# Attention, FFN and gated convolution on one core: the instruction order from a list scheduler, and the first FFN matrix scaled in groups

## The chip, the cores and the metric

The kernel runs on one core of one Trainium2 chip. The metric is device time in microseconds, the median of the runs shown. In the texts PE is TensorE (matmuls), DVE is VectorE, ACT is ScalarE, POOL is GpSimd and SP is the queue from which every DMA is issued. L12 is line 12 of the kernel's file.

## The reference

Attention over 4 batches, 8 heads, 576 positions and head size 64, then a layer norm with a two-layer FFN, then a gated block with a causal convolution of 5 taps:

```python
q_rot, k_rot = rotate(q), rotate(k)                     # rotary embedding
scores = q_rot @ k_rot.T / sqrt(64)
attn = softmax(scores)                                  # maximum subtracted
x = (attn @ v) as (4, 576, 512)
xn = (x - mean) / sqrt(var + 1e-6) * g_ln
x = x + relu(xn @ w_ch1) @ w_ch2                        # 512 -> 2048 -> 512
gate = sigmoid(sum_k conv_w[k] * x shifted by 4 - k)
out = (gate * (x @ w_val)) @ w_out
```

The weights arrive as float64; the FFN's two are 8 MB each.

## The kernel before

Rows are cut in 18 tiles of 128 (tile n spans batches, which have four and a half tiles each). For every matrix product each operand is split into a high and a low half (fp16, or fp32r in the scores and the gated block), and three products, high by high, high by low and low by high, are added in PSUM.

*Attention.* There are 16 pairs of heads (4 batches by 4). `schedule_prep` loads q and k of a pair (L188), multiplies by the rotary tables (`mul`, L196), adds (`add`, L200), and writes the high half on ACT (`hi`) and the low half on DVE (`lo`). V is bounded by the maximum of its sums, scaled by a power of two and split (`vabs`, `vmax`, `vscale`, `vhi`, `vlo`). A score tile is 128 query rows of one head against 576 keys: six matmuls of 288 columns with 64 contraction rows (`a_scores`, L292). The two heads of a pair sit on partitions 0 to 63 and 64 to 127, and `a_scores` issues their matmuls in turn. The 64 rows that are left of a batch are done for both heads in one diagonal tile (`qd`). So a pair has nine tiles, 144 in all. Each goes through maximum (DVE, L297), exponential (ACT, L303), high half (ACT, L305), low half (DVE, L310), a DMA transpose (SP, L312) and the product with V (PE, L331 and L334). Two PSUM buffers hold scores. Batch 0 is cut by rows in three parts, 128, 128 and 320, each for all four pairs of heads; the other batches are done pair by pair.

*Weights.* Each FFN matrix comes in eight pieces of 1 MB (`Conv`): ACT and DVE make fp32 of float64 (L391, L395, L396), PE multiplies each piece with itself (L403) to bound the column norms, and one bound over all eight pieces gives one scale (`conv_scale`). Only then are the pieces scaled into high and low halves (`conv_hi`, L437, and `conv_lo`, L441). The hidden units are computed 512 at a time.

*FFN.* A row tile is normalised once all heads of its rows are done (`ln_a`, `ln_b`, `ln_d`). `f1` makes 512 hidden units in 48 matmuls of 128 columns (L520), `relu` and `hlo` split them, and `f2` adds them to the output in 12 matmuls of 512 columns (L548). The halves of the hidden units have four buffers.

*Gated block.* It goes by two row tiles: copy (L609), DMA transpose, copy (L612), high and low half (L617, L618), taps on DVE (L631), `val` (L645) and `proj` (L662).

*What sets the order.* The program is written in slots, one for each score tile. Steps are put on an agenda with a slot and a phase (`at`), and `run_slot` issues a slot's steps by phase. How many FFN steps a slot gets is a running credit (`F_0`, `F_MIN`, `F_MAX`). After that the framework's own scheduler moves instructions by its estimate of their times, one instruction at a time, so a step's instructions need not stay together. Loads are chained to stay in order (`load_in_order`, L80), and the last products are held behind the last FFN matmul (`late_pe`).

Of the kernel before, what the change touches and what calls it, by code (L numbers as in the profile page):

```python
# [26 lines left out]
LAG, LN_AHEAD = 5, 2  # L27
W1_A, W1_S, W2_A, W2_S, W_BR = -7, 2, 14, 2, 2
F_0, F_MIN, F_TAIL, F2_LAG = 0.4, 0.1, 0.8, 4
F_MAX = 0.6  # L30
STEP, X3, GT, GV, GAP_0, GAP_1, V_LEAD = 6, 1, 6, 1, 0, 0, 3
HS_0, HS_1, HS_2, LD_LEAD, RAW, KQ = 8, 4, 6, 4, 3, 2


def pow2_below_inverse(nc, pool, bound, name):

    m = pool.tile([128, 1], F32, name=name + "_m", tag=name + "_m", bufs=1)
    nc.vector.tensor_scalar(out=m, in0=bound, scalar1=1e-30, scalar2=1.02, op0=ALU.max, op1=ALU.mult)
    nc.vector.reciprocal(out=m, in_=m)
    r = pool.tile([128, 1], F32, name=name + "_r", tag=name + "_r", bufs=1)  # L40
    nc.vector.tensor_scalar(out=r.bitcast(I32), in0=m.bitcast(I32), scalar1=0x7F800000, scalar2=None, op0=ALU.bitwise_and)
    return r


def pow2_below_inverse_root(nc, pool, bound, name):

    m = pool.tile([128, 1], F32, name=name + "_m", tag=name + "_m", bufs=1)
    nc.vector.tensor_scalar(out=m, in0=bound, scalar1=1e-30, scalar2=1.05, op0=ALU.max, op1=ALU.mult)
# [3 lines left out]
    nc.vector.tensor_scalar(out=r, in0=r, scalar1=2.0 ** 63, scalar2=None, op0=ALU.mult)  # L52
    return r
# [3 lines left out]
def kernel(ctx: ExitStack, tc: tile.TileContext, qk, v, g_ln, w_ch1, w_ch2, w_val, conv_w, w_out, rope, eye, out):  # L57
# [13 lines left out]
    QX = S - 256  # L71
    KT = conv_w.shape[1] // (2 * KD)

    agenda = {}
    last_load = []

    def load_in_order(**kw):

        with tc.issue_after(last_load[-1]) if last_load else nullcontext():
            last_load.append(nc.sync.dma_start(**kw).ins)  # L80


    count = [0, -100]

    def at(i, phase, fn):
        count[0] += 1
        assert i >= count[1], (i, count[1])
        agenda.setdefault(i, []).append((phase, count[0], fn))

    def run_slot(i):  # L90
        count[1] = i
        now = agenda.setdefault(i, [])
        while now:
            e = min(now)
            now.remove(e)
            e[2]()
        del agenda[i]
        count[1] = i + 1

    EX, PRE, SC, LO, MX, F2, PV, F1, DV, AC, PO, LD = range(12)  # L100

    L = lambda es, name, bufs, **kw: es.enter_context(tc.tile_pool(name=name, bufs=bufs, side="left", reuse_waits="tile", **kw))
    R = lambda es, name, bufs, **kw: es.enter_context(tc.tile_pool(name=name, bufs=bufs, side="right", reuse_waits="tile", **kw))

# [16 lines left out]
    sW, sF, sA = ExitStack(), ExitStack(), ExitStack()  # L121
# [4 lines left out]
    scl = wpool.tile([128, 4], F32, name="scl")  # L126
    gab = wpool.tile([128, KD], F32, name="gab")
    gmax = wpool.tile([128, 1], F32, name="gmax")
    sg = wpool.tile([128, KD], F32, name="sg")
# [11 lines left out]
    kk = [ap_k.tile([128, 4 * S], F32, name="kk", tag="kq") for _ in range(2)]  # L141

# [24 lines left out]
    prep = [None] * len(parts)  # L167
    base = [next(j for j, y in enumerate(parts) if y[:2] == x[:2]) for x in parts]

    def slot_of(i):  # L170
        return i + GAP_0 * (i >= first[NP]) + GAP_1 * (i >= first[2 * NP])
# [4 lines left out]
    def schedule_prep(p, pool):  # L176
# [3 lines left out]
        st = prep[p] = {"x": [None, None]}  # L180

        two = base[p] != p

        def load(n):
            t = pool.tile([128, 2, S], F32, name="raw", tag="raw", bufs=RAW)
            st["r", n] = t[:, :, 0:S if n else nq]
            load_in_order(out=st["r", n], in_=qk[b, pr][:, n, :, slice(0, S) if n else slice(q0, q1)])

        def vload():
            st["vt"] = (pool if p < NP else ap_v).tile([128, 10, D], F32, name="vt", tag="vt", bufs=2 if p < NP else 1)  # L190
            load_in_order(out=st["vt"], in_=v[b, pr].rearrange("p c h d -> p (c h) d"))
# [10 lines left out]
        def hi(n):  # L202
            if b:
# [5 lines left out]
            elif two:  # L209
                st["x"][0] = ap_q.tile([128, 2, QX], F32R, name="qs", tag="qs", bufs=2)[:, :, 0:nq]  # L210
# [9 lines left out]
        def diag():  # L220
            if ts[0][0] is None:
                c = ts[0][1] - q0
                for h in range(2):
                    sl = slice(64 * h, 64 * h + 64)
                    nc.scalar.copy(out=qd[sl, :, sl], in_=st["x"][0].bitcast(F32)[sl, :, c:c + 64])

        def vabs():

            st["vh"] = ap_v.tile([128, 18, D + 1], F16, name="vh", tag="vh")
            nc.gpsimd.memset(st["vh"][:, :, D:], 1.0)  # L230
# [4 lines left out]
        def vmax():  # L235

            st["va"] = ps_h.tile([128, 128], F32, name="hp", tag="hp")
            nc.tensor.matmul(st["va"], upper(st["vb"]).to_broadcast([128, 128]), ident, start=True, stop=True)
            st["vm"] = ap_m.tile([128, 1], F32, name="vm", tag="vm", bufs=2)
            nc.vector.tensor_reduce(out=st["vm"], in_=st["va"], axis=AX.X, op=ALU.max)  # L240

        def vscale():
            r = pow2_below_inverse(nc, ap_m, st["vm"], "vs")
            sv = st["sv"] = ap_m.tile([128, 1], F32, name="sv", tag="sv")
            nc.vector.tensor_scalar(out=sv, in0=r, scalar1=2.0 ** 15, scalar2=None, op0=ALU.mult)
# [4 lines left out]
        def vlo():  # L250
            vh = st["vh"]
            vl = st["vl"] = ap_v.tile([128, 10, D], F16, name="vl", tag="vl")
            nc.vector.scalar_tensor_tensor(out=vl, in0=st["vt"], scalar=st["sv"], in1=vh[:, 0:10, 0:D], op0=ALU.mult, op1=ALU.subtract)  # L253
            nc.scalar.copy(out=vh[0:64, 10:18], in_=vh[64:128, 0:8])
            nc.scalar.copy(out=vh[64:128, 10:18], in_=vh[0:64, 2:10])

        i1 = slot_of(first[p])
        e = (slot_of(first[p - 1]) if p else -4) + LAG - V_LEAD * (p < NP)
        vplan = [] if two else [(e - 2, LD, vload), (e, EX, vabs), (e, LD, vmax), (e + 1, LO, vscale), (e + 1, AC, vhi), (e + 2, LO, vlo)]

        def chain(n, c):
# [74 lines left out]
    def a_out(g):  # L336
        ov = ovs.pop(g)
        n = len(groups[g])
        p = tiles[groups[g][0]][0]
        b, pr = parts[p][:2]  # L340
        xx = xs[b // 2]
        lead = tiles[groups[g][0]][1] is None
        w = n + lead
        rd = ap_m.tile([128, 6], F32, name="rd", tag="rd")
        nc.vector.tensor_scalar(out=rd[:, 0:w], in0=ov[:, 0:w, D], scalar1=1e-9 * P_SCALE, scalar2=prep_v(p)["sv"], op0=ALU.add, op1=ALU.mult)
        nc.vector.reciprocal(out=rd[:, 0:w], in_=rd[:, 0:w])
        if lead:
            p0 = 64 * (b % 2)
            for h in range(2):
                r = slice(64 * h, 64 * h + 64)  # L350
                nc.scalar.activation(out=xx[p0:p0 + 64, 4, (2 * pr + h) * D:(2 * pr + h + 1) * D], in_=ov[r, h, 0:D], func=ACTF.Copy, scale=rd[r, h:h + 1])
        m = (n - lead) // 2
        if m:
            t0 = ((b % 2) * S + tiles[groups[g][lead]][2]) // 128
            by_head = lambda x: x.rearrange("p (t h) d -> p t h d", h=2)
            nc.vector.tensor_tensor(out=xx[:, t0:t0 + m, 2 * pr * D:2 * (pr + 1) * D].rearrange("p t (h d) -> p t h d", h=2), in0=by_head(ov[:, 2 * lead:2 * lead + 2 * m, 0:D]), in1=by_head(rd[:, 2 * lead:2 * lead + 2 * m].unsqueeze(2).to_broadcast([128, 2 * m, D])), op=ALU.mult)

    for i in range(NS):
        j = slot_of(i)
        at(j, SC, lambda i=i: a_scores(i))  # L360
        at(j, MX, lambda i=i: a_max(i))
        at(j + 1, EX, lambda i=i: a_exp(i))
        at(j + 2, LO, lambda i=i: a_lo(i))
        at(j + LAG, PV, lambda i=i: a_pv(i))
    for g, ts in enumerate(groups):
        at(slot_of(ts[-1]) + LAG + 1, LO, lambda g=g: a_out(g))


    def upper(x):

        return x.bitcast(BF16).rearrange("p (n two) -> p n two", two=2)[:, :, 1]

    class Conv:

        def __init__(self, scratch, src, out, bound=None):
# [85 lines left out]


    fst = {}
    tail = {}  # L470
    fpool = {}

    def ffn_start():
# [332 lines left out]
```

## Time and profile before

| | us |
|---|---|
| median of 3 runs (lowest to highest) | 780.15 (778.78 to 783.21) |
| span of the profiled execution | 777.0 |
| PE busy | 709.5 |
| DVE busy | 605.7 |
| ACT busy | 432.0 |

The profiled execution shows its span, from the first to the last instruction; its time around the span is not given. A busy time is the union of an engine's instructions. Matmuls overlap in the pipeline, so a busy PE is not PE at its peak, and the spacing of blocks in the chain of waits says more than a matmul's mean. In the table by stretch the columns are the stretch and its length, each engine's busy time with its number of instructions, the granted TensorE clock, the busy share of the 16 DMA engines, and GB/s. In the groups by line they are line, engine, operation, tiles, shapes and count, then busy time and mean ns of one, then the idle time ahead and what ended it.

### The profile page before, as it was taken

The page shows a single profiled execution, that of the slowest core. Times are in us where ns is not written, and L with a number is a line of the kernel's source. Part 1 is how long each engine was busy: PE and PEld are TensorE (multiplying, and loading weights), DVE is VectorE, ACT ScalarE, POOL GpSimd, SP SyncE. Part 2 cuts the span into 40 slices and gives each one's busy share as a digit, 9 for nine tenths or more (in the row PEclk, how much of TensorE's full clock was granted, in tenths as well). Part 3 has the DMA queues.
Part 4 walks back from the last instruction along what each step waited for, and adds up shares of the span by engine and source line. Part 5 has one row for each costly group of instructions (what it writes and reads, how often), then busy time and mean ns, then how long its engine had stood idle before and what let it go on. Part 6 is the DMA issues. An engine that isn't in the chain of part 4 may idle for free.

```text
span 777.0 us, 19132 instructions
## 1 busy us (share of the span) xinstructions
PE 709.5 (91%) x7996; PEld 560.5 (72%) x7996; DVE 605.7 (78%) x1202; ACT 432.0 (56%) x749; POOL 15.4 (2%) x39
## 2 busy tenths in 40 slices
PE   2466777999999899999999999999999999999997
PEld 1345675686777778677777768777777778778886
DVE  6989999899788799766758886665688744659994
ACT  3678757877577667464545565564363322334553
POOL 0000000000000001000000100000100000000000
PEclk9999998999999999999999999999999999999999
DMA  7999897596898867775746676656475311202311
GB/s 251 300 268 273 252 232 157 102 184 118 173 185 179 146 126 119 162 142 96 155 73 145 113 159 115 98 84 93 79 242 83 42 21 35 55 1 59 97 63 55
DMA packets 225847, 103.62 MB, mean 133 GB/s; under 512 B 210528, under 2 KB 213600, under 8 KB 224736
## 3 DMA queue, kind: packets, MB, share of 16 engines
q1 hardware_dynamic: 225760, 102.39, 61.1%
q8 instruction: 63, 1.03, 0.6%
q14 instruction: 24, 0.20, 0.1%
HBM read 45.73 MB, written 4.72 MB: 65 GB/s over the span
## 4 chain that ended last, share of the span: by engine, by line
PE 58%; DVE 18%; DMA 15%; issue 4%; ACT 4%; SPq 1%; POOL 0%; ACTq 0%; DVEq 0%; POOLq 0%
PE acc L548 18%; PE hp L520 16%; PE sc L292 8%; PE po L662 5%; PE pv L645 5%; DMA pT<-p 4%; DMA raw<-in_qk_dram 4%; PE ov L331 4%; DVE nmx L297 3%; DVE p L310 2%; PE ov L334 2%; DVE raw L196 1%; DMA tx<-rope_sb 1%; DVE wall L396 1%; DMA r<-in_moe_w_val_dram 1%
## 5 line engine op out<-in xcount | busy, mean ns | idle before, releaser
L520 PE MATMUL hp<-xT,wall 128*128 128x128 f16 x3456 | 214.5, 220 | 2.8 <-DVE hl L538 1.3
L520 PEld LDWEIGHTS <-wall 128*128 128x128 f16 x3456 | 199.4, 98 | 17.7 <-issue 8.7
L548 PE MATMUL acc<-wall,hh 128*128 128x512 f16 x544 | 163.1, 381 | 0.2 <-DVE x L552 0.2
L303 ACT ACTIVATE p<-sc,nmx 128x576 f32<-128x576 f32 x144 | 103.9, 737 | 86.4 <-DVE nmx L297 82.8
L310 DVE SCALAR_TENSOR_TENSOR p<-p,p 128x576 f16<-128x576 f32 x144 | 106.8, 753 | 52.1 <-ACT p L305 51.6
L297 DVE TENSOR_REDUCE nmx<-sc 128x1 f32<-128x576 f32 x144 | 105.6, 751 | 8.1 <-PE sc L292 7.7
L305 ACT ACTIVATE p<-p 128x576 f16<-128x576 f32 x144 | 95.6, 679 | 27.7 <-DMA pT<-p 25.8
L548 PE MATMUL acc<-wall,hl 128*128 128x512 f16 x272 | 103.1, 379 | 0.3 <-DVE hl L538 0.3
L331 PE MATMUL ov<-vh,pT 128*128 128x65 f16 (+1 forms) x1296 | 90.3, 201 | 12.9 <-DMA pT<-p 3.8
L331 PEld LDWEIGHTS <-pT 128*128 128x128 f16 x1296 | 79.2, 101 | 25.0 <-issue 16.4
L548 PEld LDWEIGHTS <-hh 128*128 128x128 f16 x544 | 49.3, 98 | 53.0 <-issue 4.5
L538 DVE SCALAR_TENSOR_TENSOR hl<-hp,hh 128x512 f16<-128x512 f32 x68 | 46.5, 686 | 36.3 <-ACT hh L532 36.2
L292 PE MATMUL sc<-kq 64*128 64x288 f32 x576 | 71.8, 309 | 0.8 <-ACT p L303 0.7
L532 ACT ACTIVATE hh<-hp 128x512 f16<-128x512 f32 x68 | 40.0, 591 | 57.2 <-PE hp L520 56.9
L334 PE MATMUL ov<-vl,pT 128*128 128x64 f16 (+1 forms) x720 | 69.9, 201 | 1.3 <-DVE vl L253 1.2
L631 DVE SCALAR_TENSOR_TENSOR gt<-xT,cw,gt 128x256 f32<-128x256 f32 (+10 forms) x192 | 69.3, 423 | 0.2
L292 PEld LDWEIGHTS sc<-kq 64*128 64x128 f32 x576 | 55.6, 184 | 7.5 <-ACT p L303 1.3
L334 PEld LDWEIGHTS <-pT 128*128 128x128 f16 x720 | 54.3, 101 | 4.3 <-issue 0.3
L196 DVE TENSOR_TENSOR raw<-raw,rope_sb 128x1152 f32<-128x1152 f32 (+2 forms) x40 | 44.5, 1116 | 10.5 <-DMA raw<-in_qk_dram 10.5
L548 PEld LDWEIGHTS <-hl 128*128 128x128 f16 x272 | 26.6, 98 | 31.6 <-DVE hl L538 0.5
L662 PE MATMUL po<-woh,gv 128*128 128x512 f32 x144 | 48.4, 402 | 0.3 <-ACT x L665 0.3
L292 PE MATMUL sc<-kx,qs 64*128 64x288 f32 x144 | 32.9, 394 | 11.9 <-ACT p L303 11.0
(114 smaller groups left out, 930.9 us busy)
## 6 DMA issues: line engine op xcount, KB each, us to landing
raw<-in_qk_dram SPq DMA_DIRECT2D x28, 576.0 KB, 4.7
wall<-in_moe_w_ch_dram SPq DMA_DIRECT2D x8, 1024.0 KB, 7.7
kk<-in_moe_w_ch_dram SPq DMA_DIRECT2D x8, 1024.0 KB, 5.6
vt<-in_v_dram SPq DMA_DIRECT2D x16, 320.0 KB, 3.0
out_dram<-x SPq DMA_DIRECT2D x18, 256.0 KB, 2.2
pT<-p SPq DMA_TRANSPOSE x144, 3.6
r<-in_moe_w_val_dram SPq DMA_DIRECT2D x4, 512.0 KB, 6.0
r<-in_moe_w_out_dram SPq DMA_DIRECT2D x4, 512.0 KB, 4.6
```

The source lines that it names most:

```text
L196: nc.vector.tensor_tensor(out=a, in0=a, in1=t, op=ALU.mult)
L292: nc.tensor.matmul(live[i + e][:, half, 0:HS], lw[rows, a], xk[rows, k, half * HS:(half + 1) * HS], start=(n == 0), stop=(n == 2))
L297: nc.vector.tensor_reduce(out=nmx, in_=sc[:, :, 0:HS], axis=AX.XY, op=ALU.max, negate=True)
L303: nc.scalar.activation(out=p32.rearrange("p (e n) -> p e n", e=2), in_=sc[:, :, 0:HS], func=ACTF.Exp, bias=nmx)
L305: nc.scalar.activation(out=p16[:, 0], in_=p32, func=ACTF.Copy, scale=P_SCALE)
L310: nc.vector.scalar_tensor_tensor(out=p16[:, 1], in0=p32, scalar=P_SCALE, in1=p16[:, 0], op0=ALU.mult, op1=ALU.subtract)
L331: nc.tensor.matmul(o, pT[:, c], vh[:, 2 * c + hs:2 * c + hs + nh], start=(c == 0), stop=(c == 8))
L334: nc.tensor.matmul(o[..., 0:D], pT[:, c], vl[:, 2 * c + hs:2 * c + hs + nh], start=False, stop=False)
L520: nc.tensor.matmul(hp[:, j], w1[:, u, wl * 512 + o:wl * 512 + o + 128], xT[:, xl * KD + c], start=(i == 0), stop=(i == 3 * KD - 1))
L548: tail["last"] = nc.tensor.matmul(st["acc"], lw[:, j], w2[:, f + j, lo * 512:lo * 512 + 512], start=(f + j == 0 and i == 0), stop=(f + j = ...
L631: nc.vector.scalar_tensor_tensor(out=gt[:, c0:c1], in0=xT[:, c, HALO + c0 - s:HALO + c1 - s], scalar=col(KT - 1 - s), in1=gt[:, c0:c1], op ...
L662: nc.tensor.matmul(po, lw[:, d, sl], rx[:, d, :], start=(n == 0), stop=(n == 3 * KD - 1))
```

## The change

The slots, the agenda and the credit go. Every step is now registered with a planner (`Plan.step`): its engine, an assumed time, a rank, the steps it comes after, the buffers it takes and uses, and the bytes if it is a transfer. `Plan.run` plays the engines forward: of the engines it takes the one whose next step can start first, and on that engine, among the steps ready by then (within `NEAR`), the one of lowest rank. Attention steps rank by their tile, FFN steps rank behind them (f1 1000, f2 900), relu, layer norm and FFN output ahead of them, and val and proj ahead of f1 and f2. The list that results is written out under `tc.manual_schedule()`, so the instructions stand as the planner has them and the framework moves none. The diff in its core:

```diff
-    agenda = {}
-    def at(i, phase, fn):
-        agenda.setdefault(i, []).append((phase, count[0], fn))
...
+class Plan:
+    LAG = {"PE": 0.22, "DVE": 0.12, "ACT": 0.2, "POOL": 0.15, "SP": 1.9, "": 0.0}
+    RATE, NEAR, AHEAD = 313.0, 0.15, 2.0
...
+        while len(done) < len(self.steps):
+            best = None
+            for eng, xs in todo.items():
+                now = max(free.get(eng, 0.0), wire - self.AHEAD if eng == "SP" else 0.0)
+                can = [(r, x) for x in xs for r in [ready(x)] if r is not None]
+                if not can:
+                    continue
+                t = max(now, min(r for r, x in can))
+                x = min((x for r, x in can if r <= t + self.NEAR), key=lambda x: (x.rank, x.order))
+                t = max(t, ready(x))
+                if best is None or t < best[0]:
+                    best = (t, eng, x)
+            x.end = t + x.time
+            if x.size:
+                x.end = wire = max(wire, x.end) + x.size / self.RATE * 1e-3
...
+    TURN = 330000
+    dve = lambda n: 0.07 + n / 960
+    act = lambda n: 0.095 + n / 1200
...
+            x = plan.step(PE, 0.85 if h is None else 1.08, R_SC + i, lambda i=i: a_scores(i), after=..., takes=ss, ...)
...
+    order = plan.run(dict(kq=kkb))
+    with tc.manual_schedule():
+        for x in order:
+            x.fn()
```

Batches 0 and 1 are cut in rows, each part for all four pairs of heads before the next; batches 2 and 3 stay pair by pair:

```diff
         if b == 0:
-            cuts = [(c, c + 128, [(0, c), (1, c)]) for c in (0, 128)] + [(256, S, [(None, c4)] + [(h, c) for c in (256, 384) for h in range(2)])]
+            cuts = [(c, c + 128, [(0, c), (1, c)]) for c in (0, 128, 256)] + [(384, S, [(None, c4), (0, 384), (1, 384)])]
+        elif b == 1:
+            cuts = [(0, 192, [(None, c4), (0, 64), (1, 64)])] + [(c, c + 128, [(0, c), (1, c)]) for c in (192, 320, 448)]
```

The first FFN matrix is loaded in pieces of 1024 hidden units by 256 rows. Two pieces have a bound and a scale of their own; the hidden units of 512 have the scale of their group, and the second matrix takes the ratio of the group's scale to the least of the four (`s1`, `srt`, `s2`). The second matrix keeps one bound over its eight pieces. The safety factors of the bounds are all 1.08, applied once, and powers of two are multiplied in where the scale is used:

```diff
-        m = wpool.tile([128, 1], F32, name=f"wm{w}")
-        nc.vector.tensor_reduce(out=m, in_=bound[w], axis=AX.X, op=ALU.max)
...
+        ne = 1 if w else 4
+        per = 8 // ne
+        for e in range(ne):
...
+    def conv_turn(w, e):
+        nc.tensor.matmul(o, upper(m).to_broadcast([128, 128]), ident, start=True, stop=True)
...
+        r = pow2_below_inverse_root(nc, wpool, m, 1.08 if w else gmax, f"w{w}{e}")
+        if w == 0:
+            nc.vector.tensor_scalar(out=sg[:, e], in0=g_sb, scalar1=r, scalar2=ROOT * W1_SCALE, op0=ALU.mult, op1=ALU.mult)
```

So 16 halves of 512 columns are scaled for the first matrix where there were 8 of 1024. The arithmetic of the tiles, the buffers of scores, transposes and hidden units, and the number of matmuls in f1, f2, scores, value products, val and proj stay.

Three places show what moved. On PE, in attention, two heads of one pair before (`sc` are score tiles, `hp` a bound of V, `acc` the FFN output):

```order
L292 MATMUL sc_3316<-kq_2703 128x288 x6
L238 LDWEIGHTS vb_3311
L238 MATMUL hp_3357<-ident_62,vb_3311 128x128
L292 MATMUL sc_3317<-kq_2703 128x288 x6
L548 LDWEIGHTS hh_3313
L548 MATMUL acc_2825<-wall_72,hh_3313 128x512
```

and a pair in the changed order:

```order
L443 MATMUL sc_3587<-kx0_68,qs_3192 128x288
L443 MATMUL sc_3588<-kx0_68,qs_3192 128x288
L443 MATMUL sc_3587<-kx0_68,qs_3192 128x288
L443 MATMUL sc_3588<-kx0_68,qs_3192 128x288
L443 MATMUL sc_3587<-kx0_68,qs_3192 128x288
L443 MATMUL sc_3588<-kx0_68,qs_3192 128x288
```

Before, one head's six stand together and other work stands between the two heads in many pairs; now the twelve always alternate (the six rows above go on in the same way).

On DVE, in the start, around a scaling of the first matrix (`wall<-wall,sg`), before:

```order
L395 TENSOR_SCALAR wall<-wall 128x1024
L346 RECIPROCAL rd<-rd 128x2
L396 SCALAR_TENSOR_TENSOR wall<-kk,wall 128x1024
L356 TENSOR_TENSOR x_67<-ov,rd 128x128
L441 SCALAR_TENSOR_TENSOR wall<-wall,sg 128x2x512
L297 TENSOR_REDUCE nmx<-sc 128x1
L486 BN_STATS bs<-x_67 128x6
```

and now:

```order
L626 TENSOR_SCALAR sg<-g_sb,w_r 128x4
L627 TENSOR_SCALAR s_74<-w_r 128x1
L465 SCALAR_TENSOR_TENSOR p_432<-p_413,p_432 128x576
L308 TENSOR_TENSOR raw<-raw,rope_sb 128x2x128
L648 SCALAR_TENSOR_TENSOR wall<-wall,sg 128x512
L312 TENSOR_TENSOR raw<-raw 128x128
L448 TENSOR_REDUCE nmx<-sc 128x1
L648 SCALAR_TENSOR_TENSOR wall<-wall,sg 128x512
L330 SCALAR_TENSOR_TENSOR qs<-raw,qs 128x128
L590 TENSOR_SCALAR wall<-wall 128x1024
L591 SCALAR_TENSOR_TENSOR wall<-wall 128x1024
```

Before, the scaling begins while pieces of the second matrix (`kk`) are converted; now the first group is scaled while later pieces of the first matrix are still to come (the last two rows).

At the end of DVE's order, before (`gt` and `gv` are the gate and its halves, `pv` the val product):

```order
L648 TENSOR_TENSOR gt_11726<-pv_11781,gt_11726 128x256
L631 SCALAR_TENSOR_TENSOR gt_11797<-xT3_11640,cw_9299,gt_11797 128x256
L631 SCALAR_TENSOR_TENSOR gt_11804<-xT3_11640,cw_9299,gt_11804 128x256
L648 TENSOR_TENSOR gt_11797<-pv_11811,gt_11797 128x256
L650 TENSOR_TENSOR gv1_11764<-gt_11719,gv0_11763 128x256
```

and now (`xT3` and `xl3` are the transposed tile and its low half, `acc` the last FFN output):

```order
L777 SCALAR_TENSOR_TENSOR x1_4517<-acc_11757,scl_73,x1_4517 128x512
L868 COPY rope_sb_58<-x1_4517 128x1024
L880 COPY xT3_11739<-tx_11718 128x2x4x128
L893 TENSOR_TENSOR xl3_11972<-xT3_11739,xh3_11971 128x1024
L908 SCALAR_TENSOR_TENSOR gt_11974<-xT3_11739,cw_9124,gt_11974 128x256 x4
L908 SCALAR_TENSOR_TENSOR gt_11977<-xT3_11739,cw_9124,gt_11977 128x256 x4
L926 TENSOR_TENSOR gt_11974<-pv_11987,gt_11974 128x256
```

Before, taps and gates of several row tiles alternate up to the last product, and no FFN output is among them; now the last FFN output is followed by the copy, the halves and the taps of the last tile, with no row of another tile between.

## Rows read from the trace of the kernel before

**Rows 1.** The page, part 1: busy time, share of the span, instructions

```profile
PE 709.5 (91%) x7996; PEld 560.5 (72%) x7996; DVE 605.7 (78%) x1202; ACT 432.0 (56%) x749; POOL 15.4 (2%) x39
```

**Rows 2.** Busy time by stretch; columns as told under the profile above

```profile
0.00:160.50 160.50, 107.10 (x1052) 87.22 (x1053) 145.82 (x269) 108.65 (x165) 3.95 (x13) 0.97 0.85 226
...
20.00:40.00 20.00, 9.11 (x53) 7.19 (x53) 18.62 (x32) 11.93 (x19) 0.00 (x0) 1.00 1.01 315
...
160.50:300.00 139.50, 134.67 (x1683) 106.46 (x1680) 119.17 (x218) 96.32 (x165) 4.26 (x11) 0.99 0.86 162
300.00:562.00 262.00, 259.11 (x3454) 200.40 (x3453) 184.88 (x344) 142.18 (x245) 5.97 (x13) 1.00 0.63 115
...
480.00:540.00 60.00, 60.00 (x794) 46.42 (x793) 38.15 (x70) 35.45 (x59) 0.00 (x0) 1.00 0.59 91
...
562.00:768.50 206.50, 204.24 (x1795) 163.28 (x1793) 155.37 (x375) 83.77 (x174) 1.18 (x2) 1.00 0.28 68
768.50:777.00 8.50, 4.39 (x19) 3.19 (x17) 0.42 (x1) 1.12 (x3) 0.00 (x0) 0.98 0.26 95
```

**Rows 3.** The chain that ended last, 340 to 360 us: start us, us, what

```profile
343.04 0.88 PE sc L292 x6
343.92 2.60 PE acc L548 x12
346.52 0.03 PE ov L331
...
346.95 2.68 PE hp L520 x48
349.63 0.98 PE sc L292 x12
```

**Rows 4.** The same chain, near 640 and 655 us

```profile
638.60 5.60 PE po L662 x24
...
654.75 2.87 PE pv L645 x24
```

**Rows 5.** PE in order of time near 234 us: start, us, instruction

```profile
233.81 1.06 PE L292 MATMUL sc<-kq 64*128 64x288 f32 x6
234.80 0.23 PE L238 MATMUL hp<-ident,vb 128*128 128x128 bf16 x1
234.96 1.07 PE L292 MATMUL sc<-kq 64*128 64x288 f32 x6
```

**Rows 6.** Line L441: duration ns least/median/most, first and last start

```profile
L441 DVE SCALAR_TENSOR_TENSOR wall<-wall,scl x8: 1275/1282/1293, 131.7 to 159.3; 128x1024 f16<-128x1024 f32 x8
```

**Rows 7.** DVE in order of time near 116 us

```profile
116.09 0.75 DVE L297 TENSOR_REDUCE nmx<-sc 128x1 f32<-128x576 f32 x1
116.76 0.28 DVE L356 TENSOR_TENSOR x<-ov,rd 128x128 f32<-128x128 f32 x1
```

**Rows 8.** Groups by line and shape on DVE and ACT

```profile
L310 DVE SCALAR_TENSOR_TENSOR p<-p,p 128x576 f16<-128x576 f32 x144 | 106.8, 753 | 52.1 <-ACT p L305 51.6
L538 DVE SCALAR_TENSOR_TENSOR hl<-hp,hh 128x512 f16<-128x512 f32 x68 | 46.5, 686 | 36.3 <-ACT hh L532 36.2
L631 DVE SCALAR_TENSOR_TENSOR gt<-xT,cw,gt 128x256 f32<-128x256 f32 x80 | 36.3, 494 | 0.1
L618 DVE TENSOR_TENSOR xl<-xT,xh 128x1024 fp32r<-128x1024 f32 x9 | 11.1, 1232 | 1.9 <-ACT xh L617 1.9
...
L303 ACT ACTIVATE p<-sc,nmx 128x576 f32<-128x576 f32 x144 | 103.9, 737 | 86.4 <-DVE nmx L297 82.8 <-DVE p L310 1.9 <-DVE rs L488 0.9
L617 ACT ACTIVATE xh<-xT 128x1024 fp32r<-128x1024 f32 x9 | 9.5, 1061 | 8.8 <-DVE xT L612 5.2 <-PE pv L645 3.6
```

**Rows 9.** DMA issues from 480 to 540 us: count, median us to landing

```profile
pT<-p SPq DMA_TRANSPOSE x18, 3.5
```

**Rows 10.** DMA issues of the whole span, the gated block's transposes

```profile
tx<-rope_sb SPq DMA_TRANSPOSE x18, 3.2
```

**Rows 11.** The last instructions, in order of time

```profile
772.69 1.08 ACT L665 ACTIVATE x<-po 128x512 f32<-128x512 f32 x2 [4.15 <-PE po L662]
```

More of the change, by code (lines that the diff above doesn't have):

```diff
@@ L220, in diag @@
         def diag():
[L221 to L227, printed above, removed]
+            c = ts[0][1] - q0
+            for h in range(2):
+                sl = slice(64 * h, 64 * h + 64)
+                nc.scalar.copy(out=qd[sl, :, sl], in_=st["x"][0].bitcast(F32)[sl, :, c:c + 64])
@@ L229, in vabs, with vabs_m @@
+        bf["ready"] = ready
+        if ts[0][0] is None:
+            bf["qd"] = Buf("qd")
+            x = plan.step(ACT, 0.5, first[p] - 1, diag, after=[bf["ql"], c_q], takes=[bf["qd"]], uses=[bf["q"]])
+            bf["dg"] = x
+        if two:
+            return
+        def vabs_m():
             st["vh"] = ap_v.tile([128, 18, D + 1], F16, name="vh", tag="vh")
             nc.gpsimd.memset(st["vh"][:, :, D:], 1.0)
+        def vabs():
             va = st["vh"][:, 0:10, 0:D].bitcast(BF16)
@@ L396, in p2 @@
             nc.vector.scalar_tensor_tensor(out=ai, in0=self.raw[:, :, 0], scalar=29, in1=ai, op0=ALU.logical_shift_right, op1=ALU.bitwise_or)
-        def p3(self):
-            o, start, stop = self.bound
-            k = self.n // 128
-            for j in range(k):
-                x = upper(self.out[:, j * 128:j * 128 + 128])
-                nc.tensor.matmul(o, x, x, start=(start and j == 0), stop=(stop and j == k - 1))
-        def schedule(self, i, after=0):
-            at(max(i - 3, count[1], after), LD, self.load)
-            at(i, AC, self.p1)
-            at(i + 1, DV, self.p2)
-            if self.bound is not None:
-                at(i + 2, PRE, self.p3)
     wfu = wf.rearrange("p u n -> p (u n)")
@@ L432, in w_scale, with products @@
-    def w_scale(w, g):
-        return scl[:, 1:2] if w else sg[:, g % KD:g % KD + 1]
-    def conv_hi(w, g):
+    bound, wmax = {}, {}
+    def products(w, o, x, start, stop):
+        if w not in bound:
+            bound[w] = ps_a.tile([128, 1, 128], F32, name=f"bound{w}", tag="acc")
+        k = x.shape[1] // 128
+        for j in range(k):
+            y = upper(x[:, j * 128:j * 128 + 128])
+            nc.tensor.matmul(bound[w][:, 0], y, y, start=(start and j == 0), stop=(stop and j == k - 1))
@@ L436, in conv_hi, with halves @@
+    def halves(w, g):
         u = 16 * w + 2 * g
[L437 to L466 removed]
@@ new lines, with start_tail @@
+    for n, y in pend_hid.items():
+        for o in rows[n]:
+            o.deps.append(y)
+    tail = {}
+    def start_tail():
+        sA.close()
+        tail["wp"] = R(ctx, "w3", 1)
+        tw = R(sT, "tw", 1)
+        tail["raw"] = [tw.tile([128, 1024], F32, name=f"r3_{j}") for j in range(4)]
+        tail["tmp"] = [tw.tile([128, 512], F32, name=f"t3_{j}") for j in range(4)]
+        tail["cw"] = tail["wp"].tile([128, KT * KD], F32, name="cw")
+        for nm in ("wv", "wo"):
+            tail[nm] = tuple(tail["wp"].tile([128, KD, DM], F32R, name=nm + s) for s in "hl")
@@ L685 @@
-    nc.sync.dma_start(out=rope_sb, in_=rope)
-    nc.sync.dma_start(out=g_sb, in_=g_ln)
-    nc.sync.dma_start(out=ident, in_=eye.bitcast(BF16))
-    nc.gpsimd.memset(qd.bitcast(F32), 0.0)
-    nc.scalar.activation(out=gab, in_=g_sb, func=ACTF.Abs)
-    gt0 = ps_h.tile([128, KD, 128], F32, name="gt0", tag="hp")
-    for c in range(KD):
-        nc.tensor.matmul(gt0[:, c], upper(gab[:, c:c + 1]).to_broadcast([128, 128]), ident, start=True, stop=True)
-    nc.vector.tensor_reduce(out=gmax, in_=gt0, axis=AX.XY, op=ALU.max)
```

736 lines of the change are left out of this document (464 added, 272 removed).

## The prediction

> **What bounds the kernel now.** I read the page's busy line first: TensorE (PE) is busy for 91% of the span, VectorE (DVE) for 78%, ScalarE for 56% [rows 1]. That is an average over stages that differ, so the table by stage comes next [rows 2]. Until 160.5 us PE is busy for 107 us, and DVE for 146 us: the start belongs to DVE. From 160.5 to 768.5 us PE is busy for 598 of 608 us, while DVE falls to 71% and the DMA share from 0.86 to 0.28.
>
> PE's busy time counts matmuls that overlap, so I price PE's work by the spacing of its blocks instead, from the chain of waits [rows 3, 4]: 48 first-layer matmuls (one `f1`) 2.68 us, 12 second-layer ones (one `f2`) 2.60, the scores of two heads interleaved 0.98, those of a diagonal tile 0.88, the value product of a tile 0.43 (346.52 to 346.95; a diagonal tile twice that), 24 matmuls of `val` 2.87, 24 of `proj` 5.60. Over the program: 72 f1 193.0, 72 f2 187.2, 64 head pairs 62.7, 16 diagonals 14.1, value products 68.8, val 51.7, proj 50.4, and 8 for the small matmuls: 636 us.
>
> The kernel before does not get its pairs at that price. In its PE order only 31 of 64 pairs alternate between the two heads. In the other 33 one head's six matmuls run, then something else, then the other's, and each six takes 0.99 us [rows 5]: 233.81 to 234.80, and 234.96 to 235.97. Two sixes cost 1.98 us for 0.98, so 33 us more, 669 us in all, and PE stands idle or slow for 777.0 - 669 = 108 us. I split this at one mark, the end of the last scaling of the second FFN matrix on DVE, which starts at 159.3 us [rows 6]. Counted along the order, the blocks before the mark are worth 75 us: 85.5 us are lost before it, 18.8 between it and 768.5 us, and 4.1 in the last 8.5 us (4.4 us of work there).
>
> **The change, part by part.**
>
> *Start.* All FFN work waits for weights that DVE must convert, and DVE is what runs out. A DVE instruction costs its mean less about 0.07 us of overlap: the 0.75 us instruction at 116.09 is followed by the next at 116.76 [rows 7]. I count DVE's instructions ahead of the mark in both orders. The changed order has three more low halves of hidden units (3 x 0.61) and one more tile through maximum and remainder (2 x 0.68), 3.2 us by [rows 8]; the rest (three more low halves of V, one more layer norm, five more output groups, 23 more one-column instructions for four bounds instead of one, queries cut in 128 and 192 rows, 16 halves of 512 for 8 of 1024) nets to 8.7 us, an estimate from the same spacing. So 11.9 us more DVE work stand ahead of the mark; at the first half of that scaling the difference is 16.3 us. DVE idles for 14.7 of the first 160.5 us [rows 2], half of it before any data is there; I let the finer pieces fill two of the rest and take 10. The ends are 5 (they fill most of it) and 20 (each piece adds a wait). The mark moves from 160.5 to 170.5 us. In return PE has done 76 us by then, with 8 f1 blocks ahead of the first f2 instead of 4. The first f1 stands earlier, after 14 us of PE work instead of 23, but an f2 needs the second matrix, whose scaling is still one bound over all eight pieces; the hidden halves then fill their ring and PE waits. Starting the FFN sooner is therefore covered, and worth nothing by itself.
>
> *DMA in the start.* Ahead of the last second-matrix load, SP's queue holds 23.5 MB and 17 transposes before, 24.4 MB and 26 transposes after. A plain load moves at 315 GB/s with the DMA share at 1.01; 18 transposes and one small load from 480 to 540 us take a share of 0.59 of 60 us, so 1.9 us for each transpose [rows 2, 9]. That makes 107 us before and 127 after. DVE reaches the conversion of that piece after 130.6 us of its work, about 140 us, so the 20 us are hidden by some 13. The Trainium skill (DMA: Bandwidth & Descriptors, Latency and other measured facts) gives a DMA transpose 261 GB/s, which for the 0.295 MB of a tile (128 x 1152 x 2 bytes) would be 1.13 us, an estimate from that page. By it the margin would be over 30 us; the measured rows decide and leave the rival below a small chance.
>
> *Pairs.* In the changed PE order all 64 pairs alternate: 33 us of PE work go. Of the 33 split pairs 13 stand ahead of the mark, where PE is not the bound and their time buys nothing; 20 stand behind it, where PE is, and these 20 us are the main gain. A pair now waits until both score buffers are free. From scores to the second exponential a pair needs about 1.0 + 0.68 + 0.68 + 0.74 us [rows 3, 8] and hand-overs, under 4 us, and pairs follow each other every 6 us, so I put the wait at 0; if it were the other end, most of the gain, 16 us, would come back.
>
> *The middle.* The remaining PE work is 636 - 76 = 560 us. Before, 18.8 us of 608 were lost in this stretch. The changed order spreads the FFN evenly: from the mark to the 80th tile it holds 142 us of PE work and 143 of DVE work, nearly equal, where the kernel before had 134.7 and 119.2 busy us in 139.5 [rows 2]. Less starving and more coupling: I keep 18.8. The ends are 8 (DVE kept full) and 43 (the first rival).
>
> *Tail.* f1 and f2 alternate with val and proj as before, and PE stays the bound there (204 of 206.5 us [rows 2]). The ring depths (one `x3`, one `gv`) stay, so I add nothing; a wait for the low half ahead of each of eight val groups would be up to 6 us, and lies within the middle's upper end.
>
> *End.* Before, the last f2 was followed by 68 us of saved-up val and proj. In the changed order val goes first wherever it can, and behind the last f2 only four val and two proj blocks stand (11.3 us of PE work). They need the chain of the last tile: FFN output and copy (1.4 us by DVE's spacing), the transpose to landing 3.2 [rows 10] and its issue, the second copy 0.7, the high half 1.06, the low half 1.23 [rows 8], hand-overs 1: val can start some 9 us after the last f2. DVE has the 16 taps still to do, 0.42 each by their spacing [rows 8], and holds the last val product until 18.5; remainders 1.2, two proj 5.6, and output as before, from 772.69 to the end at 777.0 [rows 11]: 29.8 us, 18.5 of them idle, for 4.1 before. The bounds are 14 (the low half comes before the taps throughout) and 26 (proj waits once more for each remainder).
>
> **The sum**, against the profiled span: 170.5 to the mark + 560 + 18.8 + 18.5 = 767.8 us, 9 less. What lies around the span of that execution is not shown; the median of the timed runs is 780.15, 3.2 above the span, and I add the same: 771 us.
>
> **Rivals.**
>
> 1. DVE becomes the bound of the middle (slower). Up to the 80th tile the forecast asks 97% of DVE. In the first 160.5 us it ran at 91%, half of its idle time being the wait for first data, but at 119.2 of 139.5, 85%, when PE was as full [rows 2]. All engines take their instructions in order, so one late exponential holds the line. At 85% the 143 us take 168 instead of 148: +20, 793 us. It decides below about 92%. Against it: there PE, not DVE, was what was waited for.
> 2. The planned order fits better than I credit: waits in the middle at 8, the mark at 168, the end at 15: 636 + 92 + 8 + 15 = 751 span, 754 us. For it: from 300 to 562 us PE was busy for 259.1 of 262 us [rows 2], so such a density exists here.
> 3. The pairs save nothing, because the wait for two buffers at once takes it (16 us: 787 us). For it: two buffers for two heads. Against: 2 us of spare per pair.
> 4. The 1.9 us transposes make the second matrix late by up to 10 us: 781 us.
>
> **How the numbers follow.** 0.5% is about what a measurement of this kernel can tell from no change, 776.2 to 784.1 us. Forecast 0.46 (765 to 779: of it 0.34 faster, 0.12 same), rival 2 0.23 (faster), rival 1 0.20 (slower), rival 3 0.06 (0.05 slower, 0.01 same), rival 4 0.05 (same). Faster 0.57, same 0.18, slower 0.25. The range, 748 to 792, takes rival 2 and most of rival 1.
>
> **What would show it.** Score matmuls of heads in twelves of 1.0 us throughout, in half the busy time of those before; the last second-matrix scaling on DVE near 170 us; PE full from about 175 us; the last f2 some 30 us from the end, with a gap of 9 us on PE behind it. Wrong: a mark after 185 us, DVE waits on ScalarE above 10% between the mark and tile 80, or PE gaps in the tail where val waits for the low half.

## The result: slower by 0.9%, with the profile after

The changed kernel takes 786.84 us (median of 5 runs, 784.96 to 788.78), the kernel before 778.78 in the same comparison: ratio 1.0094, interval 1.0065 to 1.0123. The forecast was 771 us.

The page of the changed kernel, busy time, which answers to [rows 1]:

```profile
PE 688.6 (88%) x8001; PEld 541.5 (69%) x8001; DVE 640.5 (82%) x1302; ACT 440.8 (56%) x773; POOL 16.4 (2%) x39
```

PE is busy for 20.9 us less, DVE for 34.8 us more. By stretch, as in [rows 2], the changed kernel:

```profile
0.00:187.10 187.10, 113.75 (x1269) 92.22 (x1270) 168.58 (x346) 124.17 (x202) 3.83 (x15) 0.82 0.79 207
...
187.10:300.00 112.90, 110.01 (x1430) 81.97 (x1429) 104.78 (x223) 72.36 (x130) 4.37 (x8) 0.98 0.81 148
300.00:560.00 260.00, 251.49 (x3472) 195.47 (x3469) 218.31 (x391) 167.57 (x285) 8.15 (x16) 1.00 0.77 146
...
187.10:758.80 571.70, 559.90 (x6661) 437.19 (x6660) 458.32 (x929) 309.59 (x556) 12.52 (x24) 1.00 0.59 112
758.80:785.00 26.20, 14.94 (x74) 12.14 (x72) 13.56 (x28) 7.01 (x15) 0.00 (x0) 0.80 0.11 31
```

The mark, the end of the last scaling of the second matrix, which answers to [rows 6] (line L648: duration ns least/median/most, first and last start):

```profile
L648 DVE SCALAR_TENSOR_TENSOR wall<-wall,s x8: 1273/1276/1285, 163.8 to 185.8; 128x1024 f16<-128x1024 f32 x8
```

It is at 187.1 us, against 160.5 before and 170.5 forecast. To see where the two kernels stand at one moment, PE's first groups up to 560 us, in the changed kernel:

```profile
L745 PE MATMUL hp<-xT,wall 128*128 128x128 f16 x2520 | 154.4, 222 | 2.2 <-DVE wall L648 2.2
L773 PE MATMUL acc<-wall,hh 128*128 128x512 f16 x376 | 112.8, 382 | 0.0
```

and in the kernel before:

```profile
L520 PE MATMUL hp<-xT,wall 128*128 128x128 f16 x2511 | 158.4, 221 | 1.5 <-DMA xT<-x 0.9 <-DVE wall L441 0.6
L548 PE MATMUL acc<-wall,hh 128*128 128x512 f16 x376 | 112.9, 381 | 0.0
```

With attention complete in both, they have done the same FFN work at 560 us. What the pairs gave behind the mark was lost ahead of it (12 us of PE work are missing at 187 us and made up by 400 us, by the table below), and the 8.0 us between the spans arise behind 560 us, by stretch in the changed kernel and in the kernel before:

```profile
560.00:785.00 225.00, 213.35 (x1840) 171.89 (x1837) 148.79 (x344) 76.67 (x158) 0.00 (x0) 0.98 0.21 46
```

```profile
560.00:777.00 217.00, 210.62 (x1849) 168.43 (x1846) 157.62 (x382) 84.89 (x176) 1.18 (x2) 1.00 0.28 69
```

PE idles there for 11.7 us against 6.4. The last instructions show where (chain of waits of the changed kernel, then PE in order of time with the idle time before):

```profile
756.81 2.39 PE acc L773 x11
...
759.22 0.76 DVE x L777
...
760.01 0.70 DVE rope_sb L868
...
760.73 3.04 DMA tx<-rope_sb
...
763.79 0.75 DVE xT L880
...
764.56 1.06 ACT xh L888
```

```profile
765.67 0.58 PE L921 MATMUL pv<-xh,wvh 128*128 128x256 f32 x1 [6.49 <-ACT xh L888]
```

Behind the last second-layer block stands the chain of the last tile alone. PE waits 6.5 us for it, then does nearly half of `val` at half pace (the granted clock is at the lower of its two levels), and its last `proj` block waits for DVE's taps and remainders: 26.2 us for work that is worth 11.3 us by the prices of the prediction.

### The profile page after: what moved, and what is told of

Read it like the earlier page. It is cut to its first block, busy times and chain, and to the rows that moved or that the text cites. A ratio compares the mean times of both kernels' runs of the same rounds, so it can differ in the third digit from the quotient of the medians.

```text
span 785.0 us, 19308 instructions
## 1 busy us (share of the span) xinstructions
PE 688.6 (88%) x8001; PEld 541.5 (69%) x8001; DVE 640.5 (82%) x1302; ACT 440.8 (56%) x773; POOL 16.4 (2%) x39
## 4 chain that ended last, share of the span: by engine, by line
PE 58%; DVE 23%; DMA 10%; ACT 5%; issue 4%; SPq 0%; ACTq 0%; DVEq 0%
PE acc L773 17%; PE hp L745 16%; DMA pT<-p 8%; PE po L948 6%; PE sc L443 6%; PE pv L921 5%; PE ov L489 4%; DVE p L465 3%; DVE nmx L448 3%; DVE raw L308 2%; DVE gt L908 2%; PE ov L492 2%; DVE wall L648 2%; ACT p L454 1%; DMA raw<-in_qk_dram 1%
## 5 line engine op out<-in xcount | busy, mean ns | idle before, releaser
L745 PE MATMUL hp<-xT,wall 128*128 128x128 f16 x3456 | 209.6, 222 | 2.2 <-DVE wall L648 2.2
L489 PE MATMUL ov<-vh,pT 128*128 128x65 f16 (+1 forms) x1296 | 97.4, 203 | 29.2 <-DMA pT<-p 23.0
L489 PEld LDWEIGHTS <-pT 128*128 128x128 f16 x1296 | 81.2, 101 | 47.2 <-DMA pT<-p 32.7
L460 ACT ACTIVATE p<-p 128x576 f16<-128x576 f32 x144 | 97.4, 681 | 4.4 <-DMA pT<-p 1.6
L908 DVE SCALAR_TENSOR_TENSOR gt<-xT,cw,gt 128x256 f32<-128x256 f32 (+4 forms) x192 | 72.1, 413 | 5.5 <-ACT gt L899 2.9
L492 PEld LDWEIGHTS <-pT 128*128 128x128 f16 x720 | 54.8, 102 | 3.4
L921 PE MATMUL pv<-xh,wvh 128*128 128x256 f32 x144 | 45.2, 314 | 6.5 <-ACT xh L888 6.5
L308 DVE TENSOR_TENSOR raw<-raw,rope_sb 128x1152 f32<-128x1152 f32 (+2 forms) x56 | 46.8, 835 | 3.6 <-DMA raw<-in_qk_dram 3.6
L443 PE MATMUL sc<-kx,qs 64*128 64x288 f32 x336 | 38.2, 344 | 12.0 <-ACT p L454 12.0
L921 PE MATMUL pv<-xl,wvh 128*128 128x256 f32 x144 | 41.8, 290 | 1.1 <-DVE xl L893 1.1
```

Source lines behind the costliest of these rows:

```text
L443: nc.tensor.matmul(live[i + e][:, half, 0:HS], lw[rows, a], xk[rows, k, half * HS:(half + 1) * HS], start=(n == 0), stop=(n == 2))
L460: nc.scalar.activation(out=p16[:, 0], in_=p32, func=ACTF.Copy, scale=P_SCALE)
L489: nc.tensor.matmul(o, pT[:, c], vh[:, 2 * c + hs:2 * c + hs + nh], start=(c == 0), stop=(c == 8))
L492: nc.tensor.matmul(o[..., 0:D], pT[:, c], vl[:, 2 * c + hs:2 * c + hs + nh], start=False, stop=False)
L745: nc.tensor.matmul(hp[:, j], w1[:, u, wl * 512 + o:wl * 512 + o + 128], xT[:, xl * KD + c], start=(i == 0), stop=(i == 3 * KD - 1))
L908: nc.vector.scalar_tensor_tensor(out=gt[:, c0:c1], in0=xT[:, c, HALO + c0 - s:HALO + c1 - s], scalar=col(KT - 1 - s, c), in1=gt[:, c0:c1], ...
```

## The experiments

All are edits of the changed kernel. Ratios are to the kernel before on the same chip; the difference is to 1.0094, in us of 780. "PE work" is counted as in the prediction: the blocks done by a moment, from the groups up to it, by their prices; where a cell is empty it was not counted.

| | ratio, interval | us against the change | mark | PE work at 187 / 400 / 440 / 560 us |
|---|---|---|---|---|
| before | 1 | -7 | 160.5 | 87.3 / 274.1 / 313.8 / 426.9 |
| the change | 1.0094, 1.0065 to 1.0123 | 0 | 187.1 | 75.4 / 273.7 / 312.5 / 427.7 |
| e1_split | 1.0236, 1.0202 to 1.0270 | +11 | 187.9 | |
| e2_early | 0.9978, 0.9957 to 0.9999 | -9 | 165.4 | 84.0 / 282.1 / 309.9 / 425.1 |
| e3_onebound | 0.9971, 0.9950 to 0.9992 | -10 | 186.7 | 76.1 / - / - / 427.2 |
| e4_tail | 0.9957, 0.9928 to 0.9986 | -11 | 188.0 | 73.2 / 273.1 / 312.0 / 427.5 |
| e5_warm | 1.0345, 1.0282 to 1.0409 | +20 | 201.8 | |
| e6_apart | 1.0681, 1.0636 to 1.0727 | +46 | 194.1 | |
| e7_coarser | 0.9954, 0.9930 to 0.9979 | -11 | 184.6 | 77.0 / 279.4 / 316.4 / 434.4 |
| e8_warm_tail | 1.0235, 1.0186 to 1.0285 | +11 | 200.6 | |
| e9_unchain | 0.9969, 0.9940 to 0.9999 | -10 | 185.4 | 76.9 / 279.4 / 317.4 / 436.3 |
| e10_coarser_tail | 0.9877, 0.9826 to 0.9928 | -17 | 184.5 | 76.9 / - / - / 434.3 |
| e11_all | 0.9865, 0.9807 to 0.9922 | -18 | 182.0 | 78.6 / - / - / 436.4 |
| e12_all_one | 0.9795, 0.9744 to 0.9846 | -23 | 180.8 | 81.9 / 281.4 / 319.6 / 438.8 |

**Do the pairs count?** e1_split makes the loop over the two heads of a pair the outer one; e6_apart also puts one matmul between them:

```diff
-        for n, (a, k) in enumerate(((1, 1), (1, 0), (0, 1))):
-            for half in range(2):
-                for e, (rows, lw) in enumerate(todo):
+        for e, (rows, lw) in enumerate(todo):
+            if e:      # in e6_apart only
+                nc.tensor.matmul(live[i + 1][:, 0, 384:512], ident, ident, start=True, stop=True)
+            for n, (a, k) in enumerate(((1, 1), (1, 0), (0, 1))):
+                for half in range(2):
```

> The changed kernel with the six matmuls of one head issued before the six of the other, in every pair; order, tiles and all else stay. Theory A (PE is what binds from the end of the last scaling of the second matrix on, and an alternating pair costs 0.98 us where two sixes cost 1.98): 64 pairs are 64 us more PE work; 16 pairs stand ahead of that mark and cost little there, 48 behind it, so about +48 us, 835 us, with the mark near 187 us as in the changed kernel. Rival B (the pairs save nothing, since a pair waits for two score buffers or DVE binds the middle): within 5 us of the changed kernel, 782 to 792 us.

> The changed kernel with the two heads' sixes of a pair issued one after the other, as in the first experiment, and one small matmul of 128 columns between them, into spare columns of the score buffer. In the first experiment a pair then took 1.36 us instead of 0.99. If the rest of the overlap goes with the matmul between them, a pair takes 2.0 us as in the kernel before. Theory A (PE binds behind the mark): 48 pairs there by 1.0 us, of which the first experiment let through about two thirds (11 of 18 us): 815 to 835 us. Rival I (a pair still overlaps): 799 us as in the first experiment.

The chain of waits of the change, of e1_split and of e6_apart, a pair each (start, us, what):

```profile
408.02 0.99 PE sc L443 x12
```

```profile
404.12 1.36 PE sc L443 x12
```

```profile
407.63 0.98 PE sc L445 x6
408.61 0.16 PE sc L442
408.77 0.99 PE sc L445 x6
```

On e1_split theory A missed (11 us came, not 48), and so did rival B, since two sixes one right behind the other still overlap by a third: 1.36 us for twice 0.99. Apart, a pair takes 2.13 us for 0.99: 48 pairs behind the mark are 55 us more PE work, and 46 us came (51.7 by the profiled spans, 7.0 of them ahead of the mark). PE does bind behind the mark, and the gain of the pairs there is real.

**Is the mark what counts?** e2_early:

```diff
-R_W1, S_W1, R_W2, S_W2 = 3, 1, 16, 2
+R_W1, S_W1, R_W2, S_W2 = 3, 1, 12, 1
```

> The changed kernel with the second matrix ranked earlier in the planner (base 16, step 2 becomes base 12, step 1), nothing else. In its order 28 maxima and 27 low halves of attention stand on DVE ahead of the last scaling of the second matrix, where the changed kernel has 36 and 34, and the prep of four transfers fewer. Theory A (the time is the mark, plus the PE work that is left then, plus some 37 us of waits): the mark moves from 187 to about 163 us, PE has some 11 us less done by then, so 24 - 11 = 13 us earlier at the end, 774 us. Rival B (DVE is short up to the end of attention; what is put off is paid back there): mark near 163 but the time within 4 us of 787. Rival C (the clock in the start, 0.59 to 0.87 from 40 to 200 us, sets the time): no change of the mark beyond 5 us.

The 9 us won lie between the forecasts, A's 13 and B's 4 at most, and the mark came at 165.4. But the lead of 8.6 us at 187 is gone at 440: from 400 to 440 us e2_early has

```profile
400.00:440.00 40.00, 33.38 (x426) 26.21 (x423) 36.60 (x65) 28.18 (x49) 1.59 (x3) 0.86 0.88 172
```

where the change has

```profile
400.00:440.00 40.00, 39.42 (x562) 30.81 (x560) 36.81 (x74) 27.66 (x49) 3.83 (x6) 1.00 0.85 145
```

The FFN had used up the rows that attention had finished: from 421 to 439 us no FFN matmul runs on PE, and the next layer norm starts at 429.2. PE waited for the next scores (3.53 us in one place, for the exponential that frees the buffer); DVE was busy for 36.6 of 40 us. This is rival B's mechanism: attention, with DVE nearly full, sets the pace, and an earlier mark is paid back. The gain arose at the end, where its order leaves more val and proj behind the last second-layer block (19.8 us of PE in its last 26.0).

**The end.** e4_tail ranks val and proj of the last two blocks behind the FFN (both lines get `+ (400 if m >= 7 else 0)`); e3_onebound has one bound for the first matrix (the diff in its core):

```diff
-        ne = 1 if w else 4
+        ne = 1
```

> The changed kernel with val and proj of the last two blocks of the gated part ranked behind the FFN instead of ahead of it. Theory A: 22.7 us of PE work of the last block but one then stands behind the last second-layer block and covers the chain of the last tile; of the 15 us that PE idles in the last 26 us some 10 go: 777 us, mark unchanged near 187. Rival E (that work can't be saved up: the single buffers of halves and gates hold the block behind, or DVE's taps are late all the same): 784 to 789 us, with the gap still behind the last second-layer block.

> The changed kernel with one bound and scale for the first matrix instead of one for each group of 512 hidden units; still 16 halves of 512 columns. It takes three chains of a maximum, a small matmul, a maximum and four to five one-column instructions from DVE ahead of the mark, and holds every first-layer block until all of the first matrix is converted. Theory A: about 4 us less DVE work ahead of the mark (187 to 183), and the eight first-layer blocks still fit in front of it: 780 to 784 us. Rival D (scaling by groups pays: the early first-layer blocks are what PE lives on in the start): first-layer blocks start later and the time goes up, 790 us or more.

e4_tail, behind its last second-layer block:

```profile
750.60:778.30 27.70, 22.31 (x122) 18.39 (x120) 15.24 (x32) 8.82 (x19) 0.00 (x0) 0.94 0.15 48
```

Theory A held: level with the change at 560 us, and PE works 22.3 of the last 27.7 us. e3_onebound hit neither of its theories: the mark did not move, PE work at 560 us is level, and the gain came behind it as in e4_tail (18.4 us of PE work stand behind its last second-layer block, for 11.3 in the change). The bounds by group gain nothing here.

**The clock of the start.** In e5_warm the loop over the nine chunks of a value product runs `range(3 if i < 40 else 1)` times.

> The changed kernel in which the value product of each of the first 40 tiles is computed three times over (the sum starts anew each time, so the result is the same): about 34 us of PE work that nobody needs, put into the time in which PE waits, in the same order. Theory F (the start is late also because PE runs at the low granted clock there: 0.59 to 0.87 from 40 to 200 us, where a pair of scores takes 1.81 us for 0.99 and a first-layer block 4.48 for 2.68, and DVE waits behind them): the clock stays near 1, DVE's idle time ahead of the mark falls from 18 to about 10 us, the mark comes at 179 and the end at 779 us. Rival G (DVE's own work sets the mark, and the clock costs nothing): mark within 3 us of 187, time 785 to 790. Rival H (the added work itself delays): later than 790.

From 40 to 100 and to 160 us, e5_warm and then the change:

```profile
40.00:100.00 60.00, 43.42 (x723) 39.93 (x723) 50.41 (x119) 32.84 (x51) 0.94 (x1) 0.80 0.68 164
100.00:160.00 60.00, 50.66 (x960) 47.24 (x957) 51.20 (x97) 33.42 (x54) 1.50 (x2) 0.89 0.97 211
```

```profile
40.00:100.00 60.00, 36.90 (x452) 32.43 (x453) 55.40 (x127) 36.10 (x56) 0.93 (x1) 0.77 0.68 172
100.00:160.00 60.00, 45.80 (x621) 40.47 (x618) 55.51 (x107) 38.00 (x64) 1.67 (x3) 0.78 0.94 230
```

The clock hardly rose (0.77 to 0.80, 0.78 to 0.89), and the added work held DVE up, which idles for 32.3 us ahead of the mark instead of 18.5: rival H. That PE's work counts in the start is shown; what the low clock costs stays open. Single executions don't settle it: of the five of the change the one at the lowest mean clock, 0.943, took 784.96 us and the one at the highest, 0.969, took 785.82, but of the 13 of the kernel before beside e9_unchain the fastest, 777.33 us, had 0.982 and the slowest, 786.63, had 0.958.

> The added value products of e5_warm and the saved-up val and proj of e4_tail together. If the clock of the start and the end are two separate losses, the gains add: 10 us from the end and what e5_warm gains, 770 us by theory F, 778 by rival G.

Both forecasts missed, since e5_warm itself lost. Against e5_warm it won 0.0110 of the ratio, 9 us: the end is a loss of its own.

**DVE's work.** e7_coarser cuts by rows more coarsely:

```diff
-cuts = [(c, c + 128, ...) for c in (0, 128, 256)] + [(384, S, ...)]
+cuts = [(c, c + 128, ...) for c in (0, 128)] + [(256, S, ...)]
...
-cuts = [(0, 192, ...)] + [(c, c + 128, ...) for c in (192, 320, 448)]
+cuts = [(0, 320, ...), (320, S, ...)]
```

A chain is here a row of DVE instructions of which each needs the result of the one right before. e9_unchain makes steps of single instructions, so that others can come between (the taps of two column blocks take turns, for one); of the output scale:

```diff
-x = plan.step(DVE, 0.24 + m * 0.14 + (0.1 if m else 0), R_OUT + ts[-1], lambda g=g: a_rd(g), ...)
+x = plan.step(DVE, 0.14, R_OUT + ts[-1], lambda g=g: a_rd(g, 0), ...)
+x = plan.step(DVE, 0.1, R_OUT + ts[-1], lambda g=g: a_rd(g, 1), after=[x], ...)
+o.append(plan.step(DVE, 0.08 + 0.14 * m, R_OUT + ts[-1], lambda g=g: a_rd(g, 2), after=[x], ...))
```

> The changed kernel with coarser cuts by rows: batch 0 in parts of 128, 128 and 320 rows as before the change, batch 1 in two parts of 320 and 256 rows instead of four (the query buffers grow from 192 to 320 columns). On DVE 22 steps fewer stand ahead of the mark: 11 output groups for 15 and 19 rotary products for 25, some 5.5 us. Theory A: the mark at 181 us; the FFN gets its rows later, and the time follows the mark if PE is not starved later: 783 us. Rival J (the fine cuts feed the FFN; without them PE starves between 187 and 300 us): 795 us or more. Rival B as it stands after the second experiment (what is won in the start is lost again before 450 us): within 3 us of 787.

> The changed kernel in which the planner has four steps cut into their single DVE instructions (output scale: sum, reciprocal, product; conversion of a piece: shift, or; layer norm's statistics; the taps of the gate), and lets a DVE step that needs the one just before it wait 0.05 us more, so that another comes between. Instructions that need the result of the one right before them: 450 in the changed order, 265 before the change, 324 here. Theory K (in such a chain an instruction gives no overlap and some 0.03 us are lost, 0.1 us together: DVE's busy time rose by 35 us though the sum of its instructions' times rose by 14): DVE's busy time falls by about 12 us, the mark comes some 5 us earlier, and the time falls as in e7_coarser, where 9 us less of DVE gave 11: 775 to 780 us. Rival L (the cut chains end later, the FFN gets its rows later): DVE's busy time falls, but the time stays within 3 us of 787 or grows.

DVE in order of time, the change and then e9_unchain:

```profile
104.11 0.21 DVE L507 TENSOR_SCALAR rd<-ov,sv 128x2 f32<-128x2 f32 x1
104.36 0.17 DVE L508 RECIPROCAL rd<-rd 128x2 f32<-128x2 f32 x1
104.56 0.29 DVE L512 TENSOR_TENSOR x<-ov,rd 128x128 f32<-128x128 f32 x1
```

```profile
105.00 0.21 DVE L510 TENSOR_SCALAR rd<-ov,sv 128x2 f32<-128x2 f32 x1
105.13 0.75 DVE L465 SCALAR_TENSOR_TENSOR p<-p,p 128x576 f16<-128x576 f32 x1
105.80 0.16 DVE L512 RECIPROCAL rd<-rd 128x2 f32<-128x2 f32 x1
```

An instruction of 0.21 us holds DVE for 0.25 where the next needs its result, and for 0.13 where it doesn't. The page of e9_unchain:

```profile
PE 686.2 (88%) x8001; PEld 542.7 (70%) x8001; DVE 623.5 (80%) x1302; ACT 441.4 (57%) x773; POOL 17.8 (2%) x39
```

The same 1302 instructions take 17.0 us less. Both experiments are 7 to 9 us ahead in PE work at 560 us and keep it, with the same 11.3 us of work behind the last second-layer block as in the change. e7_coarser beat all three of its forecasts; that B's missed says that DVE work saved is not paid back as an earlier mark is. Theory K holds for DVE's busy time and for the time, but not for the mark: it moved by 1.7 us, not 5.

**Together.**

> The coarser cuts of e7_coarser and the saved-up val and proj of e4_tail. e7_coarser was 6.7 us ahead of the changed kernel in PE work at 560 us, e4_tail was level with it there and won 10 us at the end. If these are two separate losses the gains add: 787 - 11 - 10 = 767 us. If both came from the same end, 777.

> The coarser cuts, the saved-up val and proj, and the cut chains of e9_unchain together. Theory K: DVE's chains are a loss of their own, and cutting them gives at least half of what e9_unchain gives beyond 767: 760 to 764 us. Rival L: no earlier than e10_coarser_tail.

> As e11_all, with one bound for the first matrix as in e3_onebound. e3_onebound was level with the changed kernel in PE work at 560 us and had its gain at the end, as e4_tail; where the end is mended already the bound by groups costs or gives little: within 4 us of e11_all.

The end and DVE's work add up, in full or nearly: 17 us of the 21 expected, with an interval of 13 to 21. Coarser cuts and cut chains hardly add (PE work at 560 us 434.3 and 436.4), and K's forecast for e11_all missed. It is not that the coarser cuts had left few chains, for DVE's busy time falls by 15.0 us from e10_coarser_tail to e11_all, almost as by e9_unchain alone (their pages, in this order):

```profile
PE 683.3 (89%) x8001; PEld 539.0 (70%) x8001; DVE 631.5 (82%) x1230; ACT 439.3 (57%) x761; POOL 16.7 (2%) x39
```

```profile
PE 682.0 (89%) x8001; PEld 538.2 (70%) x8001; DVE 616.5 (81%) x1230; ACT 437.5 (57%) x761; POOL 15.5 (2%) x39
```

With the coarser cuts PE was busy for 366 of the 373 us from 187 to 560 us already, for 361 in the change, so less DVE work had little left to gain there; that is argued from the shares, and no run tests it. e12_all_one is 2.1% faster than the kernel before, 1.5 to 2.6% by its interval. Its four executions (764.0 to 765.9 us) all lie below the four of e11_all (767.2 to 772.3), so the bounds by group cost time here; how much is not settled, 6 us by the medians and 1.4 by the profiled spans (764.1 and 765.5).

## Why the prediction was wrong, by its own steps

- **Start: this step failed.** It put 11.9 us more DVE work ahead of the mark, let 2 of it fill idle time, and set the mark at 170.5 (165.5 to 180.5 at its ends); measured 187.1, past the 185 that it named as a sign of being wrong: 22.8 us more busy and 3.8 more idle. The sum of the instructions' times up to the mark (groups by shape) rose by 18.6 us, from 168.1 to 186.7. I took 0.07 us of overlap off each instruction, a price read where neighbours are independent [rows 7]; for 77 more instructions that is 5.4 us more overlap. Measured, the overlap fell, from 22.3 us for 269 instructions to 18.1 for 346: 9.6 of the 10.9 us by which the busy time was missed. The planner issues a step's chain without a break. Up to the mark, 116 of DVE's instructions in the changed kernel are followed without overlap, the next starting within 0.1 us of the end, against 6 before; where there is overlap it is 0.082 us as a mean, 0.088 before. e9_unchain, with 51 such places, is busy for 3.6 us less up to its mark, so the chains do cost time; but its mark is only 1.7 us earlier. The other 5.7 us of the missed mark are idle time of DVE, and their cause stays open; the granted clock up to the mark, 0.82 against 0.97 before [rows 2], may have a part in it. The Trainium skill (Perfetto Trace Analysis, Optimizing Scalar/DVE Operations) says that the end of an instruction, the acknowledgement of its writes, overlaps with the next one. The traces agree where the next doesn't need the result (0.13 us from start to start) and not where it does (0.25).
- **DMA in the start: right.** Conversions of the second matrix waited 0.5 us in all for a load.
- **Pairs: right**, by e6_apart.
- **Middle: the size was nearly right, the reason only in part, so luck had a share.** Lost were 21.8 us from the mark to the last second-layer block, for 18.8. But the sum treated the losses behind the mark as fixed, and e2_early shows that they are not: its mark at 165.4 lies ahead of the forecast's, yet it lost some 34 us in this stretch, because PE caught up with attention, and its span was 780.1 for the forecast's 767.8. Rival 1 had this mechanism, DVE's work setting the pace of attention. In the change itself PE was still the fuller engine there (110.0 of 112.9 us from 187 to 300, DVE 93%), and most of DVE's excess fell ahead of the mark.
- **Tail: right**, PE is busy in all but 0.4 us from 560 to 759.
- **End: right in sign, 3.6 us too long**: 26.2 us for 29.8, 14.9 of them beyond the priced work for 18.5. Val began after 6.5 us, not 9, ahead of the low half.
- **The sum**: 187.1 + 549.9 of PE work + 21.8 + 26.2 = 785.0, for 767.8; the mark is 16.6 of the 17.2 us, though by e2_early an earlier mark alone would not have given them back. Two slips changed nothing: DVE's share from 160.5 to 768.5 us is 76%, and 71% that of 300 to 562 us alone [rows 2]; and 20 us more than 771 make 791 for rival 1, not 793.

## What to carry to other kernels

Price a DVE instruction by its neighbour: one that needs the result right before it gives no overlap, so a planner's step should not hold a chain. Judge a later or an earlier milestone by the work done at a common later moment in both kernels, since an early start can be paid back where another engine sets the pace. Save independent work for the end, behind the last link of the longest chain.

## What the runs showed of the hardware

Two sets of six matmuls with 64 contraction rows, on different partitions, take 0.99 us issued in turn, 1.36 one set right behind the other, and 2.13 with one full matmul between (the change, e1_split, e6_apart). In the change, after 6.5 us in which PE idled, the granted clock in the last 26 us was 0.80 as a mean (its two levels, 1.2 and 2.4 GHz, are 0.5 and 1), and `val` matmuls followed one another at 0.215 us at first and at 0.12 later on. The added products of e5_warm raised the granted clock from 40 to 100 us from 0.77 to 0.80.
